# Issuing the second chunk of first-stage weights from SyncE instead of ScalarE

## The chip, the core and the metric

The kernel runs on one core of one Trainium2 chip. The metric is the device time of the program in microseconds (us), lower is better. Every comparison below is between kernels timed in the same rounds on the same chip, unless the text says otherwise. A ratio is the mean time of one kernel's fast runs over the mean of the other's from the same rounds, so it is not quite the ratio of the medians that are quoted beside it; in the experiments it leaves out each kernel's first run, the profiled one.

Engine names: PE is TensorE, PEld its weight loads, DVE VectorE, ACT ScalarE, POOL GpSimd, SP SyncE. "SPq" is SyncE's sequencer, which issues DMAs.

## The reference

Two independent attention problems, A and B, of the same shape; the outputs are concatenated.

```python
B, Sq, D = 16, 32, 1024
Hq, Hkv, Sk, Dh = 32, 4, 512, 128
q = (x @ wq)                       # 512 x 1024 times 1024 x 4096, bf16
scores = q @ k_cache^T * Dh**-0.5  # 8 query heads share one key head
p = softmax(scores)
out = (p @ v_cache) @ wo
```

## The kernel before

The kernel is one long stream of products on PE. Everything else is arranged so that PE never waits.

**The first microseconds.** Nothing can be computed before a part of x has landed and has been transposed. So x and the first weights are loaded in small pieces, in the order of need, and PE runs 23 warm-up products on a constant meanwhile. "Chunk" is one block of 128 rows of the weights; w0 holds the weights of the first 8 heads.

```python
load_x(0, 0, TT // 2)                    # 128 KB, the first thing PE needs
load_w0(nc.sync, 0, 1, 0, NF // 2)       # chunk 0,  96 KB
load_x(0, TT // 2, TT)                   # 128 KB
load_w0(nc.sync, 0, 1, NF // 2, NF)      # chunk 0,  96 KB
load_w0(nc.scalar, 1, 2, 0, NF)          # chunk 1, 192 KB, on ScalarE's queue
load_x(2, 0, TT)                         # 256 KB, the "third part of x"
load_w0(nc.sync, 2, 3, 0, NF)            # chunk 2, 192 KB
...
warm_up(23)
transpose_x(0, 0, TT // 2)
warm_up(3)
first_heads(range(0, NF // 2), (0,), 0, TT // 2)
transpose_x(0, TT // 2, TT)
first_heads(range(NF // 2, NF), (0,), 0, TT // 2)
first_heads(range(NF), (0,), TT // 2, TT)
first_heads(range(0, NF // 2), (1,))     # the first use of chunk 1
transpose_x(2, 0, TT)
...
```

**The slots.** After the first heads, 128 slots follow; each computes one group of scores and fills the gaps with products of the q projection or of the output projection. Four slots share one group of keys (`kT`), loaded by DMA transposes on SyncE.

**The plan of the later loads.** Nearly all of them go through SyncE's queue, in program order. A weight load of 1 MB is planned 10 slots before it is needed.

```python
for j in range(2, 2 * NG // GRP):
    at(GRP * (j - 1), load_k, j)                       # keys of 4 slots
    at(GRP * (j - 1) + 2, load_v, j, 2 if j < 5 else 1)
for c4 in range(4, 16):
    need = (c4 - 2) * 4 * DC / 7.0
    at(max(0, int(need) - 10), load_wq, c4 // 8, c4 % 8)   # 1 MB
```

Of the kernel before, what the change touches and what calls it, by code (L numbers as in the profile page):

```python
# [20 lines left out]
REP = HQ // HKV  # L21
# [160 lines left out]
def kernel(  # L182
# [14 lines left out]
    nc = tc.nc  # L197
# [3 lines left out]
    DC = D // P  # L201
# [16 lines left out]
    def fast_path(ok_i):  # L218
        with ExitStack() as fctx:
# [236 lines left out]
            NF = REP - 2  # L456
            HC = DC // 2
# [7 lines left out]
            def load_x(d0, t0, t1):  # L465
                nc.sync.dma_start(
                    out=x_sb[:, t0:t1, d0 * P:(d0 + 2) * P],
                    in_=x_v[:, t0:t1, d0 * P:(d0 + 2) * P],
                )

            def load_x_transposed(d0):
                nc.sync.dma_start_transpose(
                    out=xT[0][:, d0:d0 + 2, :],
                    in_=A_x.flatten_outer_dims()[:, d0 * P:(d0 + 2) * P],
                )

            def load_w0(eng, d0, d1, h0, h1):
                eng.dma_start(
                    out=w0[d0 // HC][:, d0 % HC:(d1 - 1) % HC + 1, h0 * DH:h1 * DH],
                    in_=wq_v[:, d0:d1, h0 * DH:h1 * DH],  # L480
                )

            nc.scalar.preload_act_table_set("natural_log_exp_and_others")
            load_x(0, 0, TT // 2)
            load_w0(nc.sync, 0, 1, 0, NF // 2)
            load_x(0, TT // 2, TT)
            load_w0(nc.sync, 0, 1, NF // 2, NF)
            load_w0(nc.scalar, 1, 2, 0, NF)
            load_x(2, 0, TT)
            load_w0(nc.sync, 2, 3, 0, NF)  # L490
            load_w0(nc.sync, 3, 4, 0, NF)
            load_w0(nc.sync, 0, HC, NF, REP)
            load_w0(nc.sync, HC, HC + 2, 0, REP)
            load_x_transposed(HC)
            load_w0(nc.sync, HC + 2, DC, 0, REP)
            load_x_transposed(HC + 2)
            load_wq(0, 2)
            load_k(0)
# [165 lines left out]
    ok_i = flag.tile([1, 1], I32, name="ok_i")  # L664
    total = 2 * 2 * NG * QW
    ok = fast_path(ok_i)
    with tc.If(ok < total, preferred_fallthrough_block=True, label="general"):
        general_path(tc, problems, out_flat)
# [30 lines left out]
```

## Time and profile before

| before | value | where it is read |
|---|---|---|
| time, median of the first 3 runs | 345.85 us (345.77 to 346.26) | runs |
| span of the profiled run | 344.1 us | page |
| PE busy | 99% of the span | page, part 1 |
| first part of x: issue, landing | 0.86, 4.58 us | chain of waits |
| PE idle before the first transpose | 3.55 to 4.62 us | waits, timeline |
| PE at half rate until | 9.17 us | records of the clock, spacing of the products |
| first q product after the first heads | 21.72 us | timeline |

The page's first two rows of busy time:

```profile
span 344.1 us, 5510 instructions
...
PE 339.0 (99%) x2128; PEld 214.8 (62%) x2128; DVE 266.3 (77%) x336; ACT 186.1 (54%) x209; POOL 46.7 (14%) x206
```

The chain of waits of the kernel before, in order of time (columns: start in us, length in us, what), begins with one DMA and is PE from then on, up to the last output:

```profile
0.86 3.72 DMA x_sb<-in_A_x_dram
4.62 0.61 PE xT_ps L520 x4
...
10.01 11.87 PE q_ps L530 x55
```

The DMA view of the issues between 0.8 and 1.34 us (columns: what, issuing queue, kind, count, KB, us from issue to landing) shows the two loads that start together:

```profile
w_sb<-in_A_wq_dram ACTq DMA_DIRECT2D x1, 192.0 KB, 3.5
x_sb<-in_A_x_dram SPq DMA_DIRECT2D x1, 128.0 KB, 3.7
```

The DMA records behind this view say more: the first packet of ScalarE's queue moves at 1.92 us, the first of SyncE's at 2.64, and the packets of both are interleaved until 3.9.

The timeline of PE around its start (columns: start, length, engine, line, operation, tiles, count, and in brackets the idle time before it with what ended it):

```profile
2.60 0.95 PE L512 MATMUL q_ps<-const-bfloat16-1.0 128*128 128x128 bf16 x7
4.62 0.61 PE L520 MATMUL xT_ps<-ident,x_sb 128*128 128x128 bf16 x4 [1.07 <-DMA x_sb<-in_A_x_dram]
...
6.42 3.15 PE L530 MATMUL q_ps<-xT,w_sb 128*128 128x256 bf16 x12
9.40 0.61 PE L520 MATMUL xT_ps<-ident,x_sb 128*128 128x128 bf16 x8
```

Two things are to be seen. PE waits 1.07 us for x. And four transposes from 4.62 us take as long as eight from 9.40: PE runs at half its clock until 9.17 us. The page's row of granted clock does not show this start.

```profile
39.26 0.60 PE L358 MATMUL s_ps<-qT,kT 128*128 128x256 bf16 x4
```

There is no bracket: PE waited for nothing.

### The profile page before, as it was taken

What the parts mean: (1) busy time and instruction counts of PE and PEld (TensorE: products, weight loads), DVE (VectorE), ACT (ScalarE), POOL (GpSimd) and SP (SyncE); (2) the same over time, 40 slices, a digit from 0 to 9 for tenths busy, and PEclk for the clock granted to TensorE, in tenths of its full rate; (3) what the DMA queues carried; (4) which work ended last, traced back from release to release, by engine and by line L of the source; (5) the groups of instructions that cost most, each with busy time, mean ns of one, the idle gap of its engine ahead of it and who ended that gap; (6) DMA issues with size and microseconds to landing.
All of it is one profiled execution on the core that took longest, in us unless ns stands there. A gap on an engine that the chain in (4) does not pass through costs nothing.

```text
span 344.1 us, 5510 instructions
## 1 busy us (share of the span) xinstructions
PE 339.0 (99%) x2128; PEld 214.8 (62%) x2128; DVE 266.3 (77%) x336; ACT 186.1 (54%) x209; POOL 46.7 (14%) x206
## 2 busy tenths in 40 slices
PE   7999999999999999999999999999999999999996
PEld 6455666666666666666666666666666666666555
DVE  0046988888888889888888888888988888888540
ACT  2058667667666766666654545554455555554010
POOL 0001110011111111111002212221222100111100
PEclk9999999999999999999999999999999999999999
DMA  6999989799999998899999966998449996440001
GB/s 176 301 230 313 239 238 265 147 281 231 297 283 231 231 239 231 220 200 315 289 271 242 239 137 170 352 249 227 122 105 298 341 203 138 98 117 0 17 17 33
DMA packets 127053, 71.70 MB, mean 208 GB/s; under 512 B 75824, under 2 KB 126256, under 8 KB 127024
## 3 DMA queue, kind: packets, MB, share of 16 engines
q1 hardware_dynamic: 126352, 70.01, 83.9%
q0 software_dynamic: 384, 1.05, 0.8%
q8 instruction: 17, 0.28, 0.4%
q10 hardware_dynamic: 288, 0.26, 0.4%
q14 instruction: 12, 0.10, 0.1%
HBM read 50.86 MB, written 2.10 MB: 154 GB/s over the span
## 4 chain that ended last, share of the span: by engine, by line
PE 98%; DMA 1%; ACT 0%; issue 0%; SPq 0%; ACTq 0%
PE f_ps L321 32%; PE q_ps L302 28%; PE s_ps L358 16%; PE ob L426 16%; PE q_ps L530 4%; DMA x_sb<-in_A_x_dram 1%; PE xT_ps L520 0%; ACT o_sb L330 0%; PE q_ps L512 0%; SPq L694 0%; ACTq L330 0%
## 5 line engine op out<-in xcount | busy, mean ns | idle before, releaser
L366 ACT ACTIVATE p_sb<-s_ps,shift 128x1024 bf16<-128x1024 f32 x128 | 142.7, 1115 | 100.0 <-PE s_ps L358 82.2
L377 DVE TRANSPOSE_TENSOR_REDUCE parts<-p_sb 128x32 f32<-128x1024 bf16 x128 | 158.9, 1241 | 19.6 <-ACT p_sb L366 17.9
L321 PE MATMUL f_ps<-wo_sb,oT 128*128 128x512 bf16 (+1 forms) x544 | 131.8, 366 | 0.0
L302 PE MATMUL q_ps<-xT,wq_sb 128*128 128x512 bf16 x448 | 117.6, 379 | 0.0
L358 PE MATMUL s_ps<-qT,kT 128*128 128x256 bf16 x512 | 76.8, 273 | 0.0
L426 PE MATMUL ob<-p_sb,v_sb 128*128 128x256 bf16 x512 | 76.8, 273 | 0.0
L321 PEld LDWEIGHTS <-oT 128*128 128x128 bf16 x544 | 53.2, 98 | 36.0
L358 PEld LDWEIGHTS <-kT 128*128 128x128 bf16 x512 | 56.7, 113 | 28.5 <-DMA kT<-in_B_k_cache_dram 0.4
L302 PEld LDWEIGHTS <-wq_sb 128*128 128x128 bf16 x448 | 43.8, 98 | 31.5
L426 PEld LDWEIGHTS <-v_sb 128*128 128x128 bf16 x512 | 50.1, 98 | 20.0
L448 DVE TENSOR_TENSOR oT<-r,ob 128x512 bf16<-128x512 f32 x64 | 43.9, 687 | 22.6 <-PE ob L426 22.0
L412 DVE STREAM_TRANSPOSE r<-rall 128x512 f32<-128x512 f32 x64 | 44.2, 691 | 1.1
L310 ACT CAST qT<-q_ps 128x512 bf16<-128x512 f32 x56 | 32.7, 583 | 13.8 <-PE q_ps L302 13.8
L395 POOL COPY half<-cs 64x32 f32<-64x32 f32 x32 | 6.5, 204 | 230.1 <-DVE cs L385 230.1
L330 ACT CAST o_sb<-f_ps 128x512 bf16<-128x512 f32 (+1 forms) x17 | 9.5, 559 | 24.4 <-PE f_ps L321 16.7
L530 PE MATMUL q_ps<-xT,w_sb 128*128 128x512 bf16 (+1 forms) x70 | 16.0, 392 | 0.0
L385 DVE TENSOR_REDUCE cs<-parts 128x32 f32<-128x128 f32 x32 | 12.0, 376 | 1.1
L530 PEld LDWEIGHTS <-w_sb 128*128 128x128 bf16 x70 | 7.5, 109 | 7.2 <-issue 0.3
L407 DVE RECIPROCAL rall<-sums 128x32 f32<-128x32 f32 x32 | 10.2, 319 | 1.6 <-POOL sums L404 1.6
L555 DVE CAST qT<-q_ps 128x512 bf16<-128x512 f32 x4 | 2.8, 692 | 9.6 <-PE q_ps L530 9.5
L332 POOL DMA_DIRECT2D out_dram<-o_sb x8 | 4.6, 573 | 33.2 <-ACT o_sb L330 33.2
L396 POOL TENSOR_TENSOR half<-half,cs 64x32 f32<-64x32 f32 x32 | 7.8, 243 | 2.6
(25 smaller groups left out, 46.4 us busy)
## 6 DMA issues: line engine op xcount, KB each, us to landing
wq_sb<-in_B_wq_dram SPq DMA_DIRECT2D x8, 1024.0 KB, 6.3
wo_sb<-in_A_wo_dram SPq DMA_DIRECT2D x8, 1024.0 KB, 7.6
v_sb<-in_B_v_cache_dram SPq DMA_DIRECT2D x16, 512.0 KB, 4.6
wo_sb<-in_B_wo_dram SPq DMA_DIRECT2D x8, 1024.0 KB, 8.2
v_sb<-in_A_v_cache_dram SPq DMA_DIRECT2D x13, 512.0 KB, 4.4
wq_sb<-in_A_wq_dram SPq DMA_DIRECT2D x6, 1024.0 KB, 6.9
v_sb<-in_A_v_cache_dram SPq DMA_DIRECT2D x6, 256.0 KB, 4.2
w_sb<-in_A_wq_dram SPq DMA_DIRECT2D x2, 512.0 KB, 5.9
```

The source lines that it names most:

```text
L302: nc.tensor.matmul(ps[:], lhsT=w[:, dc, (h % 4) * DH:(h % 4 + 1) * DH], rhs=xT[pr][:, dc, :], start=(dc == 0), stop=(dc == DC - 1),)
L310: nc.scalar.copy(out=qT[pr, g][:, :, hl, :], in_=ps[:].rearrange("p (b s) -> p b s", s=SQ),)
L321: nc.tensor.matmul(ps[:, 0:width], lhsT=oT[pr, tt][:, h, :], rhs=wo_tiles[pr, nh, h // REP][:, h % REP, off:off + width], start=(h == 0), ...
L358: nc.tensor.matmul(s_ps[:, c, :], lhsT=kT[:, i % GRP, c, :], rhs=qT[pr, g][:, b, :, :].rearrange("p h s -> p (h s)"), start=True, stop=True,)
L366: nc.scalar.activation(out=p_sb[:], in_=s_ps[:], func=ACTF.Exp, bias=shift[:], scale=SCALE)
L377: nc.vector.tensor_reduce(out=parts[k][:, q, :, :].rearrange("p c h -> p (c h)"), in_=st[i]["p"][:].rearrange("p c (h s) -> p (c h) s", s=SQ),
L385: nc.vector.tensor_reduce(out=cs[:], in_=parts.pop(k)[:].rearrange("p q c h -> p q h c"), axis=AX.X, op=ALU.add,)
L407: nc.vector.reciprocal(out=rall[:, k, :], in_=quad.pop(k)[:])
L412: nc.vector.transpose(out=r[:].rearrange("p n s -> p (n s)"), in_=rall[:, k, o * 2 * REP:(o + 1) * 2 * REP] .unsqueeze(2).to_broadcast([P, ...
L426: nc.tensor.matmul(ob[j][:, q, :], lhsT=v_sb[:, i % GRP, c, :], rhs=st[i]["p"][:, c, :], start=(c == 0), stop=(c == KC - 1),)
L448: nc.vector.tensor_tensor(out=out, in0=rcp.pop(j)[:].rearrange("p (q h) s -> p q h s", h=REP), in1=ob.pop(j)[:].rearrange("p q (h s) -> p ...
L530: nc.tensor.matmul(first_q[h][:, ts], lhsT=w0[dc // HC][:, dc % HC, h * DH:(h + 1) * DH], rhs=xT[0][:, dc, ts], start=(dc == 0 and t0 == 0 ...
```

## The change

Its intent: chunk 1's weights were on ScalarE's queue to save SyncE an issue. Now SyncE issues them in turn, so that one queue alone feeds the DMA engines in the first microseconds, in the order of need.

```diff
-            def load_w0(eng, d0, d1, h0, h1):
-                eng.dma_start(
+            def load_w0(d0, d1, h0, h1):
+                nc.sync.dma_start(
                     out=w0[d0 // HC][:, d0 % HC:(d1 - 1) % HC + 1, h0 * DH:h1 * DH],
                     in_=wq_v[:, d0:d1, h0 * DH:h1 * DH],
                 )
...
             load_x(0, TT // 2, TT)
-            load_w0(nc.sync, 0, 1, NF // 2, NF)
-            load_w0(nc.scalar, 1, 2, 0, NF)
+            load_w0(0, 1, NF // 2, NF)
+            load_w0(1, 2, 0, NF)
             load_x(2, 0, TT)
```

(The other calls of `load_w0` lose their first argument, which was `nc.sync`.) PE, VectorE and GpSimd have the same instructions in the same order; ScalarE loses one DMA issue, SyncE gains it in fifth place.

More of the change, by code (lines that the diff above doesn't have):

```diff
@@ L484, in fast_path @@
             load_x(0, 0, TT // 2)
-            load_w0(nc.sync, 0, 1, 0, NF // 2)
+            load_w0(0, 1, 0, NF // 2)
             load_x(0, TT // 2, TT)
-            load_w0(nc.sync, 0, 1, NF // 2, NF)
-            load_w0(nc.scalar, 1, 2, 0, NF)
+            load_w0(0, 1, NF // 2, NF)
+            load_w0(1, 2, 0, NF)
             load_x(2, 0, TT)
-            load_w0(nc.sync, 2, 3, 0, NF)
-            load_w0(nc.sync, 3, 4, 0, NF)
-            load_w0(nc.sync, 0, HC, NF, REP)
-            load_w0(nc.sync, HC, HC + 2, 0, REP)
+            load_w0(2, 3, 0, NF)
+            load_w0(3, 4, 0, NF)
+            load_w0(0, HC, NF, REP)
+            load_w0(HC, HC + 2, 0, REP)
             load_x_transposed(HC)
-            load_w0(nc.sync, HC + 2, DC, 0, REP)
+            load_w0(HC + 2, DC, 0, REP)
             load_x_transposed(HC + 2)
```

## The prediction

> **What bounds the kernel.** TensorE. In the page PE is busy 99% of the span, and the chain of waits is 98% PE and 1% DMA. That 1% is 0.86 to 4.58 us, the first quarter of x (128 KB), which the first transposes wait for. From 4.62 us on PE runs back to back to the end, so a shift of that start moves the end one for one, provided later loads still arrive in time.
>
> **What the first microseconds show (timeline, waits, DMA records).** SyncE issues at 0.86, 1.36, 1.86, 2.33 and so on, about 0.5 us each; ScalarE issues the disputed 192 KB at 0.85. The ScalarE queue's packets start at 1.9 us, those of the first x load only at 2.6 us, though both were issued together. Lone stores at the end, on either queue, show a first packet 0.8 us after issue. So I read 0.7 to 0.9 us of x's wait as time behind ScalarE's load. Landings: ScalarE's weights 4.32, x first part 4.58, first weights 4.92, x second part 5.60, next weights 5.90, third part of x 8.08, chunk 2's weights 8.67. PE first reads chunk 1's weights at 8.1 us: they arrive 3.8 us too early. The Trainium skill (DMA: Bandwidth & Descriptors, "Issuing engines are not separate DMA queues") says that queues share the same engines and a second one saves only issue time: the packets interleaved at 2.6 to 3.9 us agree.
>
> **What changes.** One SyncE issue is added (0.47 us, like its neighbours), one ScalarE issue (0.42 us) goes; the order tool shows nothing else moved.
> - First x part: packets from about 1.8 us, landing at 3.7 to 4.1 instead of 4.58. PE starts 0.5 to 0.9 us earlier.
> - Chunk 1's weights: issued at 2.84, landing near 6.3; needed at 7.3 or later. No wait.
> - Third part of x: issued 0.5 us later but behind the same bytes, landing 7.3 to 8.3; PE, moved earlier, wants it at about 8.5. Little wait.
> - Later loads had over 1.5 us of slack (chunks 4 and 5 of xT landed at 12.4, needed near 14.8).
>
> **Clock.** Until about 9.2 us PE runs at half rate (128-column transposes 107 ns apart, then 56). The skill (TensorE: Matmul & The Clock Gate, Part 1) speaks of free-running 3.4 us windows that must be busy. A shorter hole before the transposes may let the window that ends near 5.8 us count; then up to 1 us more is gained, until PE runs into the third part of x. This may vary between runs.
>
> **Sum.** -0.7 us from the earlier start; with about one chance in three -0.5 to -0.8 more from the clock; +0.1 for later loads. I predict **345.0 us**, 344.1 to 346.1 eight times in ten; faster by over 2%: 0.01, within 2%: 0.98, slower by over 2%: 0.01.
>
> **What would show it.** First x part lands at or before 4.1; first transpose moves equally; the first x load's packets start before 2.1; chunk 1's weights land before PE asks; everything after 22 us is the same, shifted.
>
> **What would prove it wrong.** If SyncE's first packets still come at 2.6, the delay is its own and nothing is gained. If issuing at 0.5 us each starves the engines (about 220 GB/s by that spacing), PE would wait at the third part of x or at chunk 1, losing some tenths. If the clock rises a window later, the loss could reach 1.7 us.

## The result

The changed kernel took 344.44 us (median of 4 runs, 344.12 to 344.75) against 346.06 (345.77 to 346.27): ratio 0.9954, 95% interval 0.9937 to 0.9971. That is 1.6 us less, inside the predicted range. Timed twice more, on other occasions, the gain was smaller: ratios 0.9976 and 0.9972 (below). The profile after, in the same views. The page:

```profile
span 342.5 us, 5510 instructions
...
PE 337.8 (99%) x2128; PEld 213.8 (62%) x2128; DVE 266.5 (78%) x336; ACT 186.1 (54%) x209; POOL 47.1 (14%) x206
```

The DMA view of the issues between 0.8 and 1.34 us:

```profile
x_sb<-in_A_x_dram SPq DMA_DIRECT2D x1, 128.0 KB, 2.3
```

The first part of x lands 1.4 us earlier, at 3.18 us. The timeline of PE:

```profile
2.60 0.95 PE L512 MATMUL q_ps<-const-bfloat16-1.0 128*128 128x128 bf16 x7
3.35 0.63 PE L520 MATMUL xT_ps<-ident,x_sb 128*128 128x128 bf16 x4
...
4.95 1.16 PE L530 MATMUL q_ps<-xT,w_sb 128*128 128x256 bf16 x9
6.31 0.82 PE L530 MATMUL q_ps<-xT,w_sb 128*128 128x512 bf16 x3 [0.21 <-DMA w_sb<-in_A_wq_dram]
7.13 0.62 PE L520 MATMUL xT_ps<-ident,x_sb 128*128 128x128 bf16 x8
```

PE no longer waits for x: it goes from its last warm-up product straight to the first transpose. It is at full rate from 4.31 us on (nine products of 256 columns in 1.16 us; before, twelve products of 256 and 512 columns took 3.15). Now it runs into the loads that follow. In the waits of the first 70 us (columns: who waited for whom, us in total, times, longest) there are new rows for kT and w_sb, and the row for x_sb is now about the third part of x (before, it was the first part, 1.3 us):

```profile
...
PEld L358 <- DMA kT<-in_A_k_cache_dram: 1.4, 2, 0.9
...
PEld L530 <- DMA w_sb<-in_A_wq_dram: 0.7, 2, 0.5
PEld L520 <- DMA x_sb<-in_A_x_dram: 0.5, 1, 0.5
...
PE s_ps L358 <- DMA kT<-in_A_k_cache_dram: 0.4, 1, 0.4
```

The row on top is not at the start at all. Around slot 8, the first to use the third group of keys:

```profile
37.59 0.63 PE L358 MATMUL s_ps<-qT,kT 128*128 128x256 bf16 x4 [0.43 <-DMA kT<-in_A_k_cache_dram]
```

And the chain of waits now runs through SyncE's queue up to this point, instead of through PE:

```profile
26.40 0.51 SPq L246
26.91 0.04 issue
26.96 1.20 SPq L246
28.15 0.04 issue
28.20 9.35 DMA kT<-in_A_k_cache_dram
37.55 0.05 issue
37.59 0.63 PE s_ps L358 x4
```

Two 1 MB weight loads (line 246) are issued just ahead of the keys, which then take 9.35 us to land. The view by stretches of 2 us (columns: stretch, length, busy time of PE, PEld, DVE, ACT, POOL with counts, granted clock, DMA share, GB/s) shows why:

```profile
28.00:30.00 2.00, 2.00 (x13) 1.13 (x12) 1.68 (x3) 1.73 (x3) 0.03 (x1) 1.00 1.09 382
...
34.00:36.00 2.00, 2.00 (x15) 1.37 (x14) 2.00 (x3) 1.21 (x3) 0.00 (x0) 1.00 1.09 347
36.00:38.00 2.00, 1.56 (x10) 0.72 (x9) 1.57 (x3) 1.13 (x2) 0.00 (x0) 1.00 1.32 279
```

The DMA engines are full (share 1.09, from 28 to 36 us, here and in before) until the keys' turn comes, so a faster start of PE does not make the keys land earlier: 37.55 instead of 37.73 us.

### Where the time came from, and where it went

"Lead" is how much earlier than in the first profile of before (21.72 us) PE reaches the first q product after the first heads. "Given back" is what PE waits for loads after that. From that product to the last one PE needs 319.0 us when it waits for nothing (318.96 in two profiles below, 319.01 in before), so lead minus given back is the change of the whole.

| profile | x lands | PE starts | full rate from | lead | given back, and where |
|---|---|---|---|---|---|
| before | 4.58 | 4.62 | 9.17 | 0 | 0.0 |
| after, 1st | 3.18 | 3.35 | 4.31 | 2.27 | 0.71: keys at 37 and 65 us |
| after, 2nd | 3.10 | 3.35 | 6.84 | 1.79 | 1.12: keys at 65 us |
| after, 3rd | 3.12 | 3.35 | 6.03 | 1.75 | 0.89: keys at 37 us |

The lead of the first profile adds up. PE starts 1.28 us earlier. At half rate, half the time is lost: 4.55 us of it in before cost 2.28 us, 0.96 us in after cost 0.48, a gain of 1.80. New waits in the first heads, from the gaps between products, cost 0.20 + 0.37 + 0.16. Sum: 1.28 + 1.80 - 0.73 = 2.35, measured 2.27. For the third profile the same sum (half rate 2.68 us; one wait of 0.43 near 13 us) gives 1.79, measured 1.75.

### The profile page after: what moved, and what is told of

Same layout as the page of the kernel before. It is cut to its first block, busy times and chain, and to the rows that moved or that the text cites. A ratio compares the mean times of both kernels' runs of the same rounds, so it can differ in the third digit from the quotient of the medians.

```text
span 342.5 us, 5510 instructions
## 1 busy us (share of the span) xinstructions
PE 337.8 (99%) x2128; PEld 213.8 (62%) x2128; DVE 266.5 (78%) x336; ACT 186.1 (54%) x209; POOL 47.1 (14%) x206
## 4 chain that ended last, share of the span: by engine, by line
PE 88%; SPq 8%; DMA 3%; issue 0%; ACT 0%; ACTq 0%
PE f_ps L321 32%; PE q_ps L302 25%; PE ob L426 16%; PE s_ps L358 15%; SPq L276 4%; DMA kT<-in_A_k_cache_dram 3%; SPq L472 1%; SPq L478 1%; SPq L246 1%; SPq L466 0%; SPq L287 0%; ACT o_sb L330 0%; SPq L694 0%; ACTq L330 0%
## 5 line engine op out<-in xcount | busy, mean ns | idle before, releaser
L530 PE MATMUL q_ps<-xT,w_sb 128*128 128x512 bf16 (+1 forms) x70 | 14.6, 362 | 0.2 <-DMA w_sb<-in_A_wq_dram 0.2
L530 PEld LDWEIGHTS <-w_sb 128*128 128x128 bf16 x70 | 6.7, 99 | 7.2 <-DMA w_sb<-in_A_wq_dram 0.7
```

Source lines behind the costliest of these rows:

```text
L530: nc.tensor.matmul(first_q[h][:, ts], lhsT=w0[dc // HC][:, dc % HC, h * DH:(h + 1) * DH], rhs=xT[0][:, dc, ts], start=(dc == 0 and t0 == 0 ...
```

## The experiments

Two questions were open. What held x back: the bytes that ScalarE's load put in front of it, or the mere fact that a second queue started? And what is the time worth that is won at the start: does the later wait for keys really take part of it back? Line numbers of some of these kernels are one or two higher than above.

### act_tiny: a second queue with almost no bytes

```diff
+            probe = const.tile([P, 2], BF16, name="probe")
+            nc.scalar.dma_start(out=probe[:], in_=A_wq[P:2 * P, 0:2])
             load_x(0, 0, TT // 2)
```

> The changed kernel plus a load of 128 x 4 bytes issued by ScalarE at the very start, where the kernel before issued 192 KB. Theory bytes (the 192 KB were moved ahead of the first part of x): the first part of x lands at 3.1 to 3.4 us as in the changed kernel (3.18), the time is that of the changed kernel, 344.4 us within 0.4. Rival start-up (a second queue that starts beside SyncE's holds back its first packets, whatever it carries): SyncE's first packets come after 2.4 us, x lands after 3.7, time 345 us or more.

Measured: 345.06 us (344.73 to 346.24; ratio to before 0.9975, 0.9962 to 0.9989). The DMA view of the first issues:

```profile
x_sb<-in_A_x_dram SPq DMA_DIRECT2D x1, 128.0 KB, 2.2
probe<-in_A_wq_dram ACTq DMA_DIRECT2D x1, 0.5 KB, 1.7
```

SyncE's first packets came at 2.00 us and x landed at 3.06. So the start-up rival is out: a second queue does not delay x by being there. ScalarE issues a load here as in before, so being rid of that issue is not the gain either. The expected time was missed, though, by 0.3 us, and lies in the rival's range (345 or more); it is the time of the first packets and of the landing that decides. Its ratio is that of the changed kernel's two later timings (0.9976 and 0.9972, below). In this profile, of the slowest run (346.24 us), PE waited 0.85 us near 13 us for a transposed part of x and 1.28 us for keys at 38 and 66 us. An extra DMA also shifts which earlier landing each later SyncE issue waits for; that this is the cause was not tried. The unchanged third profile of after shows the same wait, of 0.43.

### act_full: a second queue with the old 192 KB

```diff
+            nc.scalar.dma_start(out=w0[1][:, 0:1, 0:NF * DH], in_=wq_v[:, HC:HC + 1, 0:NF * DH])
             load_x(0, 0, TT // 2)
```

> The changed kernel plus a load of 192 KB of the same shape as the one that was moved, issued by ScalarE at the very start (its data is loaded again later, the result stays right). Both theories, bytes and start-up: SyncE's first packets at about 2.6 us, x lands at 4.3 to 4.7 us as before, time 345.5 to 346.7 us. Rival order (the gain came from what SyncE itself does, not from taking the load off ScalarE): x lands near 3.2, time near 344.4.

Measured: 346.73 us (346.20 to 347.46; ratio 1.0026, 1.0013 to 1.0039). The DMA view of the first issues:

```profile
w_sb<-in_A_wq_dram ACTq DMA_DIRECT2D x1, 192.0 KB, 3.7
x_sb<-in_A_x_dram SPq DMA_DIRECT2D x1, 128.0 KB, 4.0
```

PE's wait for x, in the waits of the same run:

```profile
PE xT_ps L521 <- DMA x_sb<-in_A_x_dram: 1.4, 1, 1.4
```

SyncE's first packet came at 2.54 us and x landed at 4.87, a little later than expected: everything that the change had won was lost again, although SyncE's own sequence was that of the changed kernel but for the waits. (The time is a less clean measure than the landing, as this kernel also moves 192 KB more in all.) ScalarE's queue moved 144 packets in both runs, of 4 bytes in act_tiny and mostly 1536 here. So it is the bytes ahead of x, not the second queue or its number of packets, that cost.

### pool_queue: a second queue, but a little later

```diff
-            load_w0(1, 2, 0, NF)
+            nc.gpsimd.dma_start(out=w0[0][:, 1:2, 0:NF * DH], in_=wq_v[:, 1:2, 0:NF * DH])
```

> The disputed 192 KB issued by GpSimd, after its identity mask, at about 1.4 us, so that a second queue still feeds the engines, but later. Theory bytes ahead: x lands at 3.1 to 3.6 us, the third part of x about 0.5 us earlier than in the changed kernel, time within 0.4 us of it. Rival one queue alone (a second queue by itself delays SyncE's): x lands after 4.0 us and the time is 345.6 us or more.

Measured: 344.50 us (344.02 to 344.99; ratio 0.9966, 0.9953 to 0.9980), beside the changed kernel's 344.90 (0.9972): the same within the intervals. GpSimd issued at 1.57 us, its first packet moved at 2.98 us, and x landed at 3.02. So "one queue alone" is not needed, at least where the second load starts when x is almost in. But the next thing in line paid, as PE's timeline shows:

```profile
4.13 0.49 PE L530 MATMUL q_ps<-xT,w_sb 128*128 128x256 bf16 x3
5.63 0.40 PE L520 MATMUL xT_ps<-ident,x_sb 128*128 128x128 bf16 x4 [1.01 <-DMA x_sb<-in_A_x_dram]
```

The second part of x landed at 5.59 us instead of 4.15, since the 192 KB now came in front of that, and PE waited 1.01 us there. The third part of x was 0.4 us earlier (6.69 against 7.08), as expected.

### hole: the changed kernel with the idle time put back

```diff
-            warm_up(23)
+            warm_up(10)
```

> The changed kernel with 10 warm-up products in place of 23, so that PE idles about 1.3 us (1.9 to 3.2 us) before x, as long as before. Theory clock (the hole kept the clock at half rate until 9.2 us): x lands near 3.2 as in the changed kernel, but the full clock comes 2 us or more later than in it (4.3), and the time is 344.6 to 345.2 us, the earlier start of 1.3 us alone. Rival start alone (the clock has no part): time 344.4 us within 0.3, as the changed kernel.

Measured: 344.64 us (344.12 to 345.70; ratio 0.9957, 0.9944 to 0.9970). PE idled from about 2.2 to 3.15 us; x landed at 3.10; the full rate came at 6.12 us. That is later than in the first profile of after, but between the other two (6.84, 6.03), so this run does not separate the theories. The time does not separate them either: 344.64 lies in both expected ranges (344.6 to 345.2, and 344.1 to 344.7). The profiled run was the slowest (345.70 us): PE gave back 1.9 us of its lead for keys at 20 and 37 us.

### no_hole: the kernel before without the idle time

```diff
-            warm_up(23)
+            warm_up(36)
```

> The kernel before with 36 warm-up products in place of 23, so that PE is busy until x lands at 4.6 us. Theory clock: the full clock comes before 7.8 us instead of 9.2, and the time falls by 0.5 to 1.2 us to 344.8 to 345.6, although x lands no earlier. Rival start alone: the time is 346.0 to 346.4, as before or 0.2 worse for the later end of the warm-up.

Measured: 346.44 us (345.99 to 346.77; ratio 1.0012, 0.9999 to 1.0025): no gain. The clock theory was right about the clock: full rate from 6.94 us instead of 9.17, and a lead of 1.02 us although PE started 0.11 us later. It was wrong about the time, since 1.6 us went to a wait for the third group of keys, which landed at 39.81 us in this profile:

```profile
PE s_ps L358 <- DMA kT<-in_A_k_cache_dram: 1.5, 1, 1.5
```

This was the first hint that the start is not the only limit. But the lead alone does not explain this wait, since in before these keys had 1.5 us of slack. They also landed 2.1 us later than in before, after the DMA engines had moved almost nothing for 1.25 us. The view by stretches, first of this run, then of before:

```profile
38.25:39.50 1.25, 0.15 (x1) 0.00 (x0) 1.22 (x2) 0.12 (x1) 0.00 (x0) 1.00 0.05 5
38.25:39.50 1.25, 1.25 (x9) 0.67 (x8) 0.84 (x2) 1.15 (x2) 0.00 (x0) 1.00 1.01 184
```

Just before, from 37.76 to 38.81 us, the DMA records have one 16 KB packet of queue 8, which the page calls "instruction". The hole profile has the same: such a packet at 19.32 us, 5 GB/s from 20.0 to 21.0, and then a wait for keys. In before such a packet at 38.51 us brought no such stop, so that the packet is the cause is not shown.

### after_again: the changed kernel, second time

No edit.

> The changed kernel once more, timed beside the next three on one chip. Both theories: 344.4 us within 0.4. The last keys of the second score group (kT of slots 8 to 11, landing 37.5 us in the first profile) make PE wait 0.4 to 1 us near 37 us.

(These keys of slots 8 to 11 are the third group of keys of the text above.)

Measured: 345.15 us (343.83 to 345.87; ratio 0.9976, 0.9955 to 0.9997). The expected time was missed by 0.3 us. PE waited 1.1 us for keys at 65 us, where they follow the transposed load of B's x on SyncE, and not at 37 us.

### margin_after: all weight loads 4 slots later

```diff
-                at(max(0, int(need) - 10), load_wq, c4 // 8, c4 % 8)
+                at(max(0, int(need) - 6), load_wq, c4 // 8, c4 % 8)
```

> The changed kernel with the 1 MB weight loads planned 6 slots ahead of their need instead of 10, so that only one of them, not two, goes through SyncE's queue ahead of the third group of keys. Theory queue backlog (part of the gain at the start is given back near 37 us, where PE waits for keys queued behind weights that are needed much later): these keys land near 34.5 us instead of 37.5, PE does not wait for them, and the time falls by 0.5 to 0.8 us to 343.6 to 344.0. Rival (the wait is not what limits the time, or another load takes its place): 344.4 within 0.2.

Measured: 345.06 us in the median, but from 344.00 to 348.29 (three runs at 344.0, others at 346.1, 346.8 and 348.3; ratio 0.9998, 0.9960 to 1.0036). The keys landed at 35.1 us and PE waited neither at 37 nor at 65 us. It waited for a group of B's keys at 186 us instead:

```profile
PEld L358 <- DMA kT<-in_B_k_cache_dram: 0.9, 1, 0.9
```

The expected time was missed in the median; the profiled run, at 344.08 us, is one of the fast three, and the slow ones were not profiled. The edit also moved the weight loads of problem B; that this is what made another point of the queue tight was not traced.

### margin_before: the same edit in the kernel before

> The same one-number edit in the kernel before, where PE never waits for these keys. Theory queue backlog: no change, 346.1 us within 0.3. If the edit helps by itself, 345.6 or less.

Measured: 347.34 us (346.43 to 347.81; ratio 1.0033, 1.0015 to 1.0052), slower, where no change was expected. The new wait at 188 us is there as well, 1.9 us of it in the profile. So this edit was no clean test of the wait at 37 us.

### no_hole_margin: before, without the idle time, weight loads 4 slots later

> The kernel before with 36 warm-up products and with the weight loads 6 slots ahead. With 36 products alone PE was 1.0 us ahead at the end of the first heads, but lost 1.6 us waiting for keys near 38 us, and the time was 346.4. Theory backlog: with the keys ahead of one weight load, the lead is kept and the time is 344.8 to 345.4 us. Rival (the earlier clock is worth nothing): 346.0 or more.

Measured: 345.87 us (345.35 to 345.99; ratio 0.9997, 0.9982 to 1.0013). Full rate from 5.63 us, a lead of 1.56 us, no wait near 38 us, but 1.07 us for B's keys at 177 us. Between the two theories; the time was missed for the same reason.

### after_third and relief_after: two loads moved instead of all

After these misses the edit was cut to the two loads that stand in front of the tight groups of keys; problem B's loads were left where they are.

```diff
-                at(max(0, int(need) - 10), load_wq, c4 // 8, c4 % 8)
+                at(max(0, int(need) - (6 if c4 in (5, 7) else 10)), load_wq, c4 // 8, c4 % 8)
```

> The changed kernel a third time, beside the next three on one chip: 344.4 to 345.2 us; x lands at 3.0 to 3.3 us; PE waits 0.4 to 1.3 us in total for keys, near 37 us or near 65 us.

> The changed kernel with two of the 1 MB weight loads (the sixth and the eighth of the first problem) 6 slots ahead of their need instead of 10, so that they queue behind the third and the sixth group of keys; the loads of the second problem stay as they are. Theory backlog: no wait for keys near 37 and 65 us and none new later; 0.4 to 1.0 us faster than the changed kernel beside it, 343.6 to 344.2 us. Rival (any load moved only moves the wait, as with all loads 4 slots later): within 0.3 us of the changed kernel, with a new wait for a load elsewhere.

Measured, in the same rounds on one chip: the changed kernel 344.90 us (344.23 to 345.01; ratio to before 0.9972, 0.9959 to 0.9986), relief_after 344.02 us (343.58 to 344.33; ratio 0.9955, 0.9941 to 0.9969). Their means differ by 0.76 us (344.77 and 344.01; from the spread of the runs, 95% interval 0.3 to 1.2), or by 0.60 without the two profiled runs (0.1 to 1.1). The expected 0.4 to 1.0 us was met. PE around slot 8 in relief_after:

```profile
36.91 0.60 PE L358 MATMUL s_ps<-qT,kT 128*128 128x256 bf16 x4
```

The keys landed at 34.43 us, no bracket is left, and no gap over 0.08 us between PE's products remains after the first heads: the whole lead of 2.35 us arrives at the end. So the wait was taken away and not moved. This version has the lowest median, 0.45% below before in its rounds (the changed kernel reached the same ratio in its first comparison, but not in these rounds).

### relief_before: the same edit in the kernel before

> The same edit in the kernel before, whose PE starts later and does not wait there: no change, within 0.3 us of before.

Measured: 346.20 us (345.15 to 346.24) beside before's 345.66; ratio 1.0013, 0.9999 to 1.0026, so no change shown (the median is 0.5 us higher, a little more than the expected 0.3). Without a lead, there is nothing for the edit to keep. (In its profile, a run of 345.15 us, the full rate came at 7.50 us by the spacing of the products, which gave this one execution a lead of 0.78 us.) So the two edits need each other: the early start makes the key loads the limit, and only then does moving weights out of their way pay.

## Why the prediction was right, point by point

- **What bounds the kernel: right.** PE, and before it the first part of x.
- **What held x back: right, but the size was too small.** The prediction said "First x part: packets from about 1.8 us, landing at 3.7 to 4.1 instead of 4.58". Packets came at 1.95, landing was at 3.18. Only the late first packet had been counted (2.64 to 1.95 us). The interleaved packets also stretched the load: from the first packet to landing it took 1.94 us before and 1.23 after. act_tiny and act_full show that it is the bytes and not the queue.
- **PE starts 0.5 to 0.9 us earlier: too small,** 1.28 us. PE then starts when its own warm-up ends; x has been there for 0.17 us.
- **Chunk 1's weights: "landing near 6.3; needed at 7.3 or later. No wait."** They landed at 6.27. In the first profile PE, at full rate, wanted them at about 5.9 and waited 0.37 us. The third part of x landed at 7.08, earlier than the predicted 7.3 to 8.3, and cost 0.16. These waits come with the faster clock, and the prediction's main case had the slow one.
- **The clock: earlier, as hoped; the chance and the size too small, the reason not shown.** "One chance in three" for 0.5 to 0.8 us. The three profiles of after reached full rate at 4.31, 6.84 and 6.03 us, against 9.17 in before; by half of the half-rate time that is 1.8, 0.5 and 0.9 us. The eight profiles with x landing by 3.2 us, those of the experiments included, reached it between 3.60 and 6.84 us. The four profiles with PE idle and x landing at 4.4 us or later (before, margin_before, act_full, relief_before) reached it between 7.5 and 9.4, the two with x as late but PE kept busy at 6.9 and 5.6. Each is one profile, and the moment varies from run to run. So an early x goes with an early clock, but the prediction's reason, a shorter hole, is not shown: the hole run put 0.98 us of idle time back and reached full rate at 6.12 us, inside the range of the profiles without it.
- **"+0.1 for later loads" and "everything after 22 us is the same, shifted": wrong.** This is the step that failed. 0.7 to 1.1 us of the lead was given back near 37 or 65 us. The prediction had looked at the slack of the loads up to 22 us. The slack of the third group of keys was 1.5 us in before, less than the lead; the keys landed 0.2 us earlier than before, so a lead of 2.27 leaves a wait of about 0.55, measured 0.60. relief_after took this wait away, and the lead was kept.
- **The sum** was right in part by luck. Two terms were too small, and one with the opposite sign was all but left out: predicted 0.85 us, measured 1.6 in the first comparison, whose profile has the earliest clock of the three, and 0.8 to 1.0 (from the ratios) in the two later ones, where the errors nearly cancel. The stated range, 344.1 to 346.1, also held the time of before, so that being inside it says little.

What stays open: why the group that is late differs from run to run (37 us in the first and third profile, mainly 65 us in the second), what stops the queue as in no_hole, and how much of the time's spread is the moment at which the clock rises.

## What to carry to other kernels

In the first microseconds, order loads by need over all queues together: whatever another queue starts beside the critical load shares its engines, and 192 KB too early cost that load 1.4 us here. When PE starts earlier, look through the whole trace for loads whose slack is smaller than the lead, since loads behind a saturated DMA queue need not move with PE (the keys landed at 37.55 us against 37.73, with PE 2.27 us ahead); here two 1 MB loads that were needed much later stood before the keys, and moving just those two kept the gain. Moving all loads by one rule only moved the wait.

## What the Trainium skill lacked or had wrong

- *DMA: Bandwidth & Descriptors*, "Issuing engines are not separate DMA queues", says that a second issuing engine only saves the sequencer's issue time, and that the DMAs interleave. The traces agree, and add the cost: to save one issue of 0.43 us on SyncE, the interleaving delayed the 128 KB load that was needed first by 1.4 us (landing 4.58 against 3.18).
- The same page, "Specifications", gives a first-byte latency of about 0.6 us for DMAs from SyncE or ScalarE without saying from when. Here the first packet of the first load came 1.1 us after its issue began (0.86 to 1.95 us), which is 0.64 us after the issue instruction ended (1.31).
- *TensorE: Matmul & The Clock Gate*, Part 1, puts the moment of full clock at about 4 us of sustained work, give or take 500 ns from run to run. That is too narrow: three profiles of one kernel, with the same warm-up, reached it at 4.31, 6.84 and 6.03 us, a spread of 2.5 us. (The same Part does warn that the number of slow products varies between runs.)
- The same page warns in Part 1 that the clock's trace events are unreliable. Agreed: one profile (relief_before) has no record of it at all, while the spacing of the products changes at 7.50 us; and the mean granted clock of all these profiles reads 0.998 to 1.0 although PE ran at half rate for its first microseconds.
- No page has a trn2 figure for what issuing a DMA transpose of this size costs the sequencer (*DMA: Bandwidth & Descriptors* has one for small tiles on "previous generations"). Here one of 128 KB kept SyncE for 1.26 us in the median of 64, and for up to 4.3 us while the engines were full, against 0.5 to 0.6 us for most plain loads of 1 MB.
